# Second half of the first tokens ahead of later weights, a new table of early steps, and the scan mask's flags sent through DRAM

## The chip, the cores and the metric

The kernel runs on one core of a Trainium2 chip, as one launch. The metric is the device time of that launch in microseconds (us); lower is better. Engines: PE is TensorE's matmul, PEld its weight load, DVE is VectorE, ACT is ScalarE, POOL is GpSimd, SP is SyncE (it issues nearly all transfers here).

## What is computed

`x` is 2048 tokens of 448 channels (`L = 2048`, `D = 448`), everything is float32. Two branches read it and a gate mixes them.

```python
g  = sigmoid((x * gate_w).sum(-1, keepdims=True))
# a: a long convolution, K built from 256 complex decays per channel
dt = exp(log_dt); A = -exp(log_A_real) + 1j * A_imag; C = (C_real + 1j * C_imag) * dt[:, None]
K  = 2 * einsum("dn,dnl->dl", C, exp((A * dt[:, None])[:, :, None] * arange(L))).real
a  = causal_convolution(x, K) + x * D_skip
# b: token shift and a channel MLP
h  = gelu(layernorm(x) @ w1)                  # 448 x 448
hs = shift(h, by channel group: +1, -1, +2, -2) @ w2
x1 = x + hs
b  = x1 + gelu(layernorm(x1) @ w3) @ w4       # 448 x 1792, 1792 x 448
out = g * a + (1 - g) * b
```

## The kernel before

**Tiles and units.** The tokens are cut into four blocks of 512 (`TB`), a block into four tiles of 128. TensorE's work is a list of 72 units: 16 units of kind "a" (block b, channel group g; `layernorm(x) @ w1` and the product with `w2`) and then 56 units of kind "d" (block b, hidden tile f of 14; the product with `w3` and the product with `w4`). For each unit `first(n)` (line 478) makes the 512-column product into a bank of PSUM, ACT takes its gelu (line 539) and a rounded copy (line 549), DVE takes the rest (`act_tail`, line 569), and `second(n)` (line 602) multiplies the result by the second weight into four accumulators. Every float32 operand is kept as a rounded high part and a low part (`xh`/`xl`, `w1h`/`w1l`, `uh`/`ul`), so each product is made of up to three: high by high, high by low, low by high. `uh` is used by the first eight of the twelve matmuls of a `second`, `ul` by the last four.

**The order of the steps.** The program order on each engine's queue is written out by hand. `begin()` runs a table, `ORDER`, for units 0 to 3 and a part of units 4 and 5. A word such as `p1:h0a` is one product of unit 1: high weight, slice 0 of the contraction, first half (`a`) of the 512 tokens; `l` is the low weight, `x` the low part of the tokens, a missing letter the whole 512. `s0:20` is one matmul of `second(0)` into accumulator 2. Other words take the next step of a small task: `w` a warm-up matmul on constants (line 902), `m2`, `m0`, `m1`, `m3` the column means of a group of `w1` (lines 930, 914, 866), `c` the centering of the weight by it (line 936, DVE), `h` and `l` its high part (line 939, ACT) and low part (line 942, DVE), `xha`/`xhb` the high part of the first and second half of the first tokens (line 955, ACT), `xla`/`xlb` the low part (line 962, DVE), `sa`, `sb` statistics of a token tile, `ra0` the reciprocal deviation, `ra` its turn into rows on PE, `hd` gelu steps, `cp` copies, `tl` low parts, `ba`, `bm` copies of those rows.

After the table a loop runs over n from 4 to 71. In turn n it issues `first(n + 2)`, the gelu of unit n + 2 and `second(n)`, and between them whatever is registered with `at(n, function, ..., when=...)`, in four lists: `before`, `after`, `between`, `late`. The list `before` runs at the turn's start, right after `act_tail(n + 1)`.

**The first loads.** Before the table `first_loads()` issues the transfers in an order written by hand: on SP and ACT, a column group of `w1` (in `w1r`), the first tokens transposed (`x0` into `r`, its first half in two parts, its second half `r[:, 4 * HW:]` later), token tiles for the statistics (`load_x`), the identity, `w2`, and the next block. Transfers take eight lanes (semaphores) in turn; a transfer is issued only when the one eight before it has landed.

**The scan branch.** The convolution is done in a short form where the decays allow it: four cumulated scans per block and channel slice with coefficients `nu`. `ssm_guard` (turn 33) computes per partition a flag `rk[:, 4:5]`, 1 if the short form is allowed there. `ssm_mask` makes one flag of the 128, writes it to `okm` and copies the coefficients `nuf` into `nu` where it is set. Before, this is a matmul with ones on PE that sums the flags over the partitions (line 734, turn 34, between `first(36)` and `second(34)`), read back by DVE. `ssm_queue` (turn 33) fills the queue of scan steps and issues the loads of the first two blocks, 1 MB each (line 744). From turn 35 (`OWN`) the scan steps run: `ssm_scale` on ACT (line 752) multiplies by `nu`, `ssm_scan` on DVE (line 757), then `ssm_sum`, and `ssm_turn` with its writes (line 775). `ssm_some` hands out scan steps per turn up to a credit. At the end, on every core engine, `okm` is read and a branch runs a general convolution if the flag is 0; with the inputs given it is not run.

**The outputs.** `done(b, j)` writes an output tile once both branches have added to it (line 579); tiles of block 0 are written in two halves. `last_two()` does the last two units and writes the last tile in two parts (line 643). After that SP waits for every lane.

Of the kernel before, what the change touches and what calls it, by code (L numbers as in the profile page):

```python
# [8 lines left out]
F32 = mybir.dt.float32  # L9
# [170 lines left out]
def mixer_and_small_steps(ctx, tc, xs, gg, okm, x, xT, xb, x0, w1, w2, w3, w4, gate, par, logdt, dskip, ident, out):  # L180
# [74 lines left out]
    def first_loads():  # L255
# [16 lines left out]
        load_w1(sp, 1)  # L272
        load_x(1, 2)
# [3 lines left out]
        sp(r[:, 4 * HW:], x0[:, 4 * HW:])  # L277
# [295 lines left out]
    def done(b, j):  # L573
        q = NT * b + j
        parts[q] = parts.get(q, 0) + 1
        if parts[q] == 2:
            for p in range(0, 128, 64 if b == 0 else 128):
                t = slice(p, p + (64 if b == 0 else 128))
                nc.sync.dma_start(out[q * 128 + t.start:q * 128 + t.stop], xs[t, q, :])
# [151 lines left out]

    def ssm_mask():
        p = ps.tile([128, 1], F32, name="misc", bufs=1)
        nc.tensor.matmul(p, one.to_broadcast([128, 128]), rk[:, 4:5], start=True, stop=True)  # L734
        nc.vector.tensor_copy(rk[:, 5:6], p)
        nc.vector.tensor_scalar(okm, rk[:, 5:6].to_broadcast([128, 16]), 127.5, None, op0=OP.is_ge)
        nc.vector.copy_predicated(nu.rearrange("p a b -> p (a b)"), okm, nuf.rearrange("p a b -> p (a b)"))
# [298 lines left out]
    def each(*calls):  # L1036

        for fn, *a in calls:
            fn(*a)
            yield  # L1040

    def more_loads():
# [8 lines left out]
        ws=each((presum,)), m0=each((presum_mean,)), w=each(*((warm_up, 1) for _ in range(5))),  # L1051
# [38 lines left out]
    w w wt xha w wt m2 w xla m2 ws c2 m0 c2 h2 h2 l2 l2 p1:h0a c0 xha xz p1:x0a sk w xz sa0 xla p1:h2a m1 c0  # L1090
    h0 xla sa1 l0 p0:x0a p1:x1a p0:h0a c1 p1:x2a h0 p1:h1a,h3a sa0 ld m3 l0 h1 p0:h3a c3 p0:x2a,l2a,l1a sa2
    p0:x1a p2:h1a sb3 p2:x0a p0:h1a,l3a,h2a h3 p2:h2a l1 p2:h3a pe xhb sb3 p3:x2a sb3 p2:x1a xhb p0:l0a
    p2:l2a p0:h0b p3:h2a xlb p2:h0a sa1 p1:h1b p2:x2a p3:h3a p2:h1b sb3 p0:h2b xlb p0:l0b sa2 p2:h0b p1:x0b
    xlb p3:x1b p0:x2b,h1b l3 p0:l1b p2:x0b wh0 p1:x2b p0:x0b p1:h3b ra0 p0:x1b ra0 p0:h3b p2:x2b ra0 p3:h1b
    xh1 p3:l3a ra0 p3:x2b p2:l0a ra0 p2:l0b ra0 xh1 p1:h0b p3:h2b ra0 p3:l2b p2:x1b ra0 p0:l3b xh1 ra0
    p2:h3b p1:x1b sk p1:h2b wl0 p0:l2b xh1 p3:l1a ra sk uf0 sk p2:l2b xl1 rm p2:l1a p3:x0b uf1 p3:l0b mu0
    p3:x0a sk p4:l1 mu0 p4:h1 sk ad1 p2:h2b hd0 p3:l3b,h0b p4:h3 hd0 mu0 p3:l2a mu1 p2:l1b bm p2:l3a mu1
    p3:h3b hd0 p3:x1a,h1a,l1b hd0 p4:l2 xl1 s0:00 hd0 s0:10 p5:h3 xl1 hd0 p4:x0 s0:01 ba p5:h0 sb7 s0:20 hd0
    hd1 p2:l3b tl0 s0:21 p3:l0a p5:x1 sb7 wh2 mu2 s0:30 p5:x0 cp1 p4:h2 sb5 p3:h0a s0:02 wh1 p4:h0 tl0 s0:11
    sb5 s0:31 tl1 hd2 s0:22 p5:h2 p4:l3 wl2 hd2 p5:h1 hd2 s0:12 sb7 p4:x1 cp2 s1:11,31 sb5 s1:20 cp2 s1:01  # L1100
    sb7 s0:32 sb5 s2:30 tl2 s1:30,10 s2:20 ra1 mu3 s2:00 s1:21 s2:22 ra1 s1:00 wl1 hd3 p4:l0 s2:10 ra1 wh3
    s2:02 ra1 s2:01 ra1 s2:31 hd3 xl1 hd3 s2:11,32,21 ra1 cp3 s2:12 ra1 p4:x2 ra1 wl3 p5:x2 s3:30 uf5 s3:20
    ra1 tl3 s3:00 rn sb9 s3:01 bn s3:12,31 ad5 s3:02 cp3 s3:21,10 mu4 s3:22,32,11 re hd4 re hd4 hd4 mu5 cp4
    re cp4 hd5 tl4 cp5 sb9 re
# [102 lines left out]
    at(34, ssm_mask, when=between)  # L1207
    at(33, ssm_queue)
    for m in (3, 2, 1, 0):
        at(OWN, ssm_scale, 0, 0, m)  # L1210
# [3 lines left out]
    with tc.manual_schedule():  # L1214
        begin()
        for n in range(4, len(units)):
# [23 lines left out]
            if n >= OWN:  # L1240
                ssm_some(n, 3.75 - (2.2 if units[n][2] == NF - 1 else 0.0) - spent)
# [59 lines left out]
```

## Time and profile before

| | before |
|---|---|
| median of three runs | 371.3 us (371.2 to 372.18) |
| time of the profiled execution | 371.42 us |
| its span, first to last instruction | 369.6 us |
| mean granted TensorE clock | 0.997 |
| PE busy | 363.9 us (98%) |
| DVE, ACT, POOL busy | 308.5, 216.1, 63.8 us |
| read from and written to DRAM | 34.74 and 11.01 MB |

The span is the time between the first and the last instruction that the profile shows; the execution's own time is 1.8 us longer. Times in the views count from the span's start. A busy PE is not PE at its peak, so holes and the spacing of equal pieces are read, not the busy share alone.

### The profile page before, as it was taken

How to read it: one execution, taken by the hardware profiler on the slowest of the kernel's cores; microseconds unless marked ns; L12 is line 12 of the kernel's file. 1: busy time of each engine (PE TensorE's matmuls, PEld its weight loads, DVE VectorE, ACT ScalarE, POOL GpSimd, SP SyncE). 2: the span in 40 equal slices, each digit the busy share in tenths (PEclk: the TensorE clock that was granted, in tenths of full speed). 3: DMA queues.
4: the chain of work that ended last, by engine and by line, in shares of the span. 5: the costliest groups of instructions: out<-in, count | busy, mean ns of one | idle time of the engine just before them, and what ended most of it. 6: DMA issues, size and time to landing. Idle time of an engine off the chain costs nothing.

```text
span 369.6 us, 5310 instructions
## 1 busy us (share of the span) xinstructions
PE 363.9 (98%) x1734; PEld 314.8 (85%) x1734; DVE 308.5 (83%) x571; ACT 216.1 (58%) x383; POOL 63.8 (17%) x176
## 2 busy tenths in 40 slices
PE   8999999999999999999999999999999999999995
PEld 5988888888888888888888888888888888888884
DVE  4999979788989997388789899997889999999433
ACT  5887678776674737944373774554656745445220
POOL 1000433000400000110014333324234324000000
PEclk9999999999999999999999999999999999999998
DMA  7994116727938064001833514367485611361213
GB/s 268 394 398 143 48 54 128 160 82 254 381 122 192 2 121 150 0 0 51 192 93 82 84 28 121 86 178 126 86 127 114 177 27 25 72 178 30 66 48 105
DMA packets 88495, 46.14 MB, mean 125 GB/s; under 512 B 67216, under 2 KB 82960, under 8 KB 87824
## 3 DMA queue, kind: packets, MB, share of 16 engines
q1 hardware_dynamic: 88032, 45.27, 45.5%
q10 hardware_dynamic: 432, 0.49, 0.4%
q8 instruction: 15, 0.25, 0.3%
q14 instruction: 16, 0.13, 0.1%
HBM read 34.74 MB, written 11.01 MB: 124 GB/s over the span
## 4 chain that ended last, share of the span: by engine, by line
PE 95%; DMA 3%; SPq 0%; ACT 0%; DVE 0%; issue 0%
PE p L478 48%; PE acc L602 45%; DMA raw<-x_in 2%; DMA w1r<-w_in 1%; PE acc L637 1%; PE misc L363 0%; PE p L637 0%; SPq L246 0%; ACT xh L955 0%; SPq L264 0%; DVE xs L626 0%; PE misc L734 0%
## 5 line engine op out<-in xcount | busy, mean ns | idle before, releaser
L539 ACT ACTIVATE uf<-p 128x512 f32<-128x512 f32 x56 | 33.5, 599 | 113.3 <-PE p L478 113.3
L478 PE MATMUL p<-xh,w3l 128*128 128x512 f32 x224 | 70.1, 394 | 0.0
L478 PE MATMUL p<-xh,w3h 128*128 128x512 f32 x224 | 70.0, 394 | 0.0
L757 DVE TENSOR_TENSOR_SCAN z<-z,carry 128x512 f32<-128x512 f32 x48 | 61.6, 1283 | 4.2 <-POOL z L751 0.5
L602 PE MATMUL acc<-w4l,uh 128*128 128x448 f32 x216 | 56.3, 366 | 0.0
L602 PE MATMUL acc<-w4h,uh 128*128 128x448 f32 x216 | 56.0, 365 | 0.0
L602 PE MATMUL acc<-w4h,ul 128*128 128x448 f32 x216 | 55.8, 364 | 0.0
L569 DVE TENSOR_TENSOR ul<-uf,uh 128x512 fp32r<-128x512 f32 x56 | 38.1, 681 | 20.0 <-ACT uh L549 19.8
L478 PEld LDWEIGHTS p<-xh,w3l 128*128 128x128 f32 x224 | 42.1, 188 | 9.8
L478 PEld LDWEIGHTS p<-xh,w3h 128*128 128x128 f32 x224 | 42.1, 188 | 6.6
L478 PE MATMUL p<-xl,w3h 128*128 128x512 f32 x168 | 47.7, 392 | 0.0
L602 PEld LDWEIGHTS acc<-w4h,uh 128*128 128x128 f32 x216 | 40.5, 188 | 6.0
L602 PEld LDWEIGHTS acc<-w4h,ul 128*128 128x128 f32 x216 | 40.6, 188 | 3.6
L602 PEld LDWEIGHTS acc<-w4l,uh 128*128 128x128 f32 x216 | 40.5, 188 | 3.4
L752 ACT ACTIVATE z<-zs,nu 128x512 f32<-128x512 f32 x64 | 42.3, 710 | 0.2 <-DVE xl L409 0.2
L478 PEld LDWEIGHTS p<-xl,w3h 128*128 128x128 f32 x168 | 31.5, 188 | 7.2
L549 ACT ACTIVATE uh<-uf 128x512 fp32r<-128x512 f32 x56 | 35.4, 633 | 1.8
L751 POOL COPY z<-carry 128x1 f32<-128x1 f32 x48 | 32.7, 692 | 16.0 <-DVE zs L763 15.9
L759 POOL COPY carry<-z 128x1 f32<-128x1 f32 x48 | 13.1, 273 | 105.1 <-DVE z L757 104.4
L344 POOL TENSOR_TENSOR t<-r 128x4 f32<-128x4 f32 (+1 forms) x5 | 3.1, 626 | 117.4 <-DVE r L343 117.4
L757 DVE TENSOR_TENSOR_SCAN z<-z,carry,zero 128x512 f32<-128x512 f32 x16 | 20.0, 1248 | 0.0
L602 PE MATMUL acc<-w2l,uh 128*128 128x448 f32 x64 | 19.9, 367 | 0.0
(207 smaller groups left out, 543.7 us busy)
## 6 DMA issues: line engine op xcount, KB each, us to landing
zs<-xT_in SPq DMA_DIRECT2D x4, 1024.0 KB, 8.1
yd<-yt SPq DMA_DIRECT2D x56, 64.0 KB, 2.0
ysb<-yd SPq DMA_DIRECT2D x16, 224.0 KB, 2.7
raw<-xb_in SPq DMA_DIRECT2D x3, 1032.0 KB, 12.6
raw<-w_in SPq DMA_DIRECT2D x3, 1024.0 KB, 5.6
xd<-xt SPq DMA_DIRECT2D x16, 192.0 KB, 2.1
xr<-xd SPq DMA_DIRECT2D x16, 192.0 KB, 3.1
raw<-w_in SPq DMA_DIRECT2D x3, 896.0 KB, 4.6
```

The source lines that it names most:

```text
L344: eng.tensor_mul(t, y, y)
L478: nc.tensor.matmul(p[:, t0:t1], (wl if w else wh)[:, k, :], (xl if x_ else xh)[:, k, o + t0:o + t1], start=(q == 0 and fresh), stop=stop i ...
L539: nc.scalar.activation(UF[n], P1[n], AF.Gelu_apprx_tanh)
L549: nc.scalar.activation(UH[n], UF[n], AF.Copy)
L569: nc.vector.tensor_sub(UL[n], uf, f32(UH[n]))
L602: nc.tensor.matmul(ACC[j], (UL if p == 2 else UH)[n][:, t], wl if p == 1 else wh, start=first_, stop=last_)
L637: nc.tensor.matmul(acc, (UL if p == 2 else UH)[m][:, t], (wl if p == 1 else wh)[:, c], start=q == last and m == n and p == 0, stop=m > n a ...
L751: nc.gpsimd.tensor_copy(z4[:, m, 0:1], carry[:, k, m:m + 1])
L752: nc.scalar.activation(z4[:, m, 1:], ZS[b][:, k, :], AF.Copy, scale=nu[:, k, m:m + 1])
L757: nc.vector.tensor_tensor_scan(z, z, up, carry[:, k, m:m + 1], OP.add, OP.add)
L759: nc.gpsimd.tensor_copy(carry[:, k, m:m + 1], z[:, TB - 1:])
```

## The change

In `first_loads` the second half of the first tokens is issued earlier, ahead of token tiles 1 to 4 and of group 3 of `w1`. The table `ORDER` is a new one, over the same tasks; it has three `w` steps instead of five. Only the first tile of block 0 is still written in two halves. The flags no longer go through PE: `ssm_tell` (turn 33, after the loads of `ssm_queue`) writes the 128 flags to DRAM, `ssm_hear` (turn 34) reads the 128 numbers back into every partition, and `ssm_mask` (now at the start of turn 35) takes their minimum on DVE. The credit per turn is 3.7 instead of 3.75.

```diff
@@ -270,11 +270,11 @@
         act(xs[:, 0, :], x[0:128])
         sp(r[:, 2 * HW:4 * HW], x0[:, 2 * HW:4 * HW])
         load_w1(sp, 1)
+        sp(r[:, 4 * HW:], x0[:, 4 * HW:])
         load_x(1, 2)
         load_x(2, 3)
         load_w1(sp, 3)
         load_x(3, 5)
-        sp(r[:, 4 * HW:], x0[:, 4 * HW:])
         sp(idt, ident)
         sp(w2r[:, 0], w2[:, 0])
         load_xt(1)
@@ -573,9 +573,10 @@
     def done(b, j):
         q = NT * b + j
         parts[q] = parts.get(q, 0) + 1
+        h = 64 if b == 0 and j < 1 else 128
         if parts[q] == 2:
-            for p in range(0, 128, 64 if b == 0 else 128):
-                t = slice(p, p + (64 if b == 0 else 128))
+            for p in range(0, 128, h):
+                t = slice(p, p + h)
                 nc.sync.dma_start(out[q * 128 + t.start:q * 128 + t.stop], xs[t, q, :])
 
     ADDED = {}
@@ -729,11 +730,21 @@
         nc.vector.tensor_scalar(rk[:, 0:4], rk[:, 0:4], RHO / L, None, op0=OP.is_le)
         nc.vector.tensor_reduce(rk[:, 4:5], rk[:, 0:4], axis=AX.X, op=OP.min)
 
+    OKB = []
+
+    def ssm_tell():
+
+        OKB.append(dr.tile([1, 128], F32, name="okd"))
+        nc.sync.dma_start(OKB[0].rearrange("o p -> p o"), rk[:, 4:5])
+
+    def ssm_hear():
+        OKB.append(big.tile([128, 128], F32, name="okb", tag="lt"))
+        row = OKB[0]
+        nc.sync.dma_start(OKB[1], bass.AP(tensor=row.tensor, offset=row.offset, ap=[[0, 128], [1, 128]]))
+
     def ssm_mask():
-        p = ps.tile([128, 1], F32, name="misc", bufs=1)
-        nc.tensor.matmul(p, one.to_broadcast([128, 128]), rk[:, 4:5], start=True, stop=True)
-        nc.vector.tensor_copy(rk[:, 5:6], p)
-        nc.vector.tensor_scalar(okm, rk[:, 5:6].to_broadcast([128, 16]), 127.5, None, op0=OP.is_ge)
+        nc.vector.tensor_reduce(rk[:, 5:6], OKB[1], axis=AX.X, op=OP.min)
+        nc.vector.tensor_scalar(okm, rk[:, 5:6].to_broadcast([128, 16]), 0.5, None, op0=OP.is_ge)
         nc.vector.copy_predicated(nu.rearrange("p a b -> p (a b)"), okm, nuf.rearrange("p a b -> p (a b)"))
 
     ZZ, ZS = {}, {}
@@ -1048,7 +1059,7 @@
         nc.sync.dma_start(dts[:, 0, :], logdt)
 
     TASKS = dict(
-        ws=each((presum,)), m0=each((presum_mean,)), w=each(*((warm_up, 1) for _ in range(5))),
+        ws=each((presum,)), m0=each((presum_mean,)), w=each(*((warm_up, 1) for _ in range(3))),
         xha=each((x_hi, 0, lh), (x_hi, 2, lh)), xhb=each((x_hi, 0, rh), (x_hi, 2, rh)),
         xla=each((x_lo, 0, 2, lh), (x_lo, 2, 3, lh), (x_lo, 3, 4, lh)),
         xlb=each((x_lo, 0, 2, rh), (x_lo, 2, 3, rh), (x_lo, 3, 4, rh)),
@@ -1087,21 +1098,20 @@
             TASKS[f"mu{n}"] = mul_ops(n)
 
     ORDER = """
-    w w wt xha w wt m2 w xla m2 ws c2 m0 c2 h2 h2 l2 l2 p1:h0a c0 xha xz p1:x0a sk w xz sa0 xla p1:h2a m1 c0
-    h0 xla sa1 l0 p0:x0a p1:x1a p0:h0a c1 p1:x2a h0 p1:h1a,h3a sa0 ld m3 l0 h1 p0:h3a c3 p0:x2a,l2a,l1a sa2
-    p0:x1a p2:h1a sb3 p2:x0a p0:h1a,l3a,h2a h3 p2:h2a l1 p2:h3a pe xhb sb3 p3:x2a sb3 p2:x1a xhb p0:l0a
-    p2:l2a p0:h0b p3:h2a xlb p2:h0a sa1 p1:h1b p2:x2a p3:h3a p2:h1b sb3 p0:h2b xlb p0:l0b sa2 p2:h0b p1:x0b
-    xlb p3:x1b p0:x2b,h1b l3 p0:l1b p2:x0b wh0 p1:x2b p0:x0b p1:h3b ra0 p0:x1b ra0 p0:h3b p2:x2b ra0 p3:h1b
-    xh1 p3:l3a ra0 p3:x2b p2:l0a ra0 p2:l0b ra0 xh1 p1:h0b p3:h2b ra0 p3:l2b p2:x1b ra0 p0:l3b xh1 ra0
-    p2:h3b p1:x1b sk p1:h2b wl0 p0:l2b xh1 p3:l1a ra sk uf0 sk p2:l2b xl1 rm p2:l1a p3:x0b uf1 p3:l0b mu0
-    p3:x0a sk p4:l1 mu0 p4:h1 sk ad1 p2:h2b hd0 p3:l3b,h0b p4:h3 hd0 mu0 p3:l2a mu1 p2:l1b bm p2:l3a mu1
-    p3:h3b hd0 p3:x1a,h1a,l1b hd0 p4:l2 xl1 s0:00 hd0 s0:10 p5:h3 xl1 hd0 p4:x0 s0:01 ba p5:h0 sb7 s0:20 hd0
-    hd1 p2:l3b tl0 s0:21 p3:l0a p5:x1 sb7 wh2 mu2 s0:30 p5:x0 cp1 p4:h2 sb5 p3:h0a s0:02 wh1 p4:h0 tl0 s0:11
-    sb5 s0:31 tl1 hd2 s0:22 p5:h2 p4:l3 wl2 hd2 p5:h1 hd2 s0:12 sb7 p4:x1 cp2 s1:11,31 sb5 s1:20 cp2 s1:01
-    sb7 s0:32 sb5 s2:30 tl2 s1:30,10 s2:20 ra1 mu3 s2:00 s1:21 s2:22 ra1 s1:00 wl1 hd3 p4:l0 s2:10 ra1 wh3
-    s2:02 ra1 s2:01 ra1 s2:31 hd3 xl1 hd3 s2:11,32,21 ra1 cp3 s2:12 ra1 p4:x2 ra1 wl3 p5:x2 s3:30 uf5 s3:20
-    ra1 tl3 s3:00 rn sb9 s3:01 bn s3:12,31 ad5 s3:02 cp3 s3:21,10 mu4 s3:22,32,11 re hd4 re hd4 hd4 mu5 cp4
-    re cp4 hd5 tl4 cp5 sb9 re
+    w w wt xha w wt m2 m2 ws c2 m0 c2 h2 xla h2 sk l2 l2 xha xz p1:h0a c0 p1:x1a xz p1:x0a,h1a sa0 xla m1 c0
+    h0 xla h0 p1:h2a l0 p1:x2a p0:x0a xhb p0:h1a c1 p0:h2a p1:h3a p0:h0a,x2a xhb p0:l0a l0 p1:h0b p0:h3a,l1a
+    xlb h1 p0:h1b ld p1:h2b p0:h2b,x1a,h0b sa0 xlb p1:h1b p2:h0a m3 l1 sa1 p2:x2b c3 p2:x0a sa2
+    p0:l2a,x0b,l1b p2:l1a sb3 p2:x1a,x0b h3 p2:l2b p1:x0b p2:h0b xlb p0:l3a pe sa1 sb3 sb3 p2:x2a p3:x2a,x0a
+    wh0 l3 p3:x0b p0:x1b p2:h2a p1:x1b sa2 p0:l2b p2:h1a sb3 wl0 p2:l0a p3:h1b p1:x2b p0:l0b p3:x2b,l3a ra0
+    xh1 p1:h3b ra0 p0:h3b,x2b ra0 p3:x1a,h3a xh1 ra0 p3:h1a ra0 p0:l3b p3:l0b ra0 p2:x1b xh1 p2:h3a ra0
+    p2:l1b ra0 p2:l0b p3:l1b ra0 p3:h0b xh1 p3:l2b sk p2:l2a,h1b sk rm uf0 sk ra xl1 uf1 p3:l0a mu0 p2:l3b
+    sk p4:l0 mu0 p2:h2b sk p2:l3a ad1 p4:h3 hd0 p4:h0,h2 hd0 mu0 mu1 p3:l2a,l3b mu1 hd0 p4:l2 p5:h2 hd0
+    p3:l1a xl1 p3:h3b hd1 s0:10 p3:x1b p5:h3 sb7 hd0 p4:l1 p3:h0a bm p4:h1 ba tl0 p5:h1 sb5 p2:h3b p5:h0 hd0
+    p3:h2a s0:00 hd0 sb7 cp1 tl0 s0:20 p3:h2b s0:11 mu2 wh2 s0:02,30,12 sb5 tl1 hd2 s0:21,01 p4:x0 sb7 hd2
+    s0:22 hd2 s1:10,00 sb5 s0:31 cp2 s1:20 sb7 s0:32 sb5 wl2 p5:x0 wh1 s1:30 p4:l3 wh3 ra1 tl2 s1:01,31
+    s2:20 ra1 s2:30 mu3 s2:00,12,22 ra1 wl1 hd3 s1:11 s2:10,02 ra1 s1:21 xl1 hd3 cp2 s2:31 hd3 s2:01,11 ra1
+    xl1 s2:32 cp3 s2:21 p5:x1 ra1 p4:x1 cp3 ra1 s3:00 ra1 wl3 p4:x2 p5:x2 s3:10 ra1 sb9 uf5 s3:30 rn tl3
+    s3:01 bn s3:31,20 ad5 s3:22,32,02 mu4 s3:12,21,11 re hd4 mu5 hd4 hd4 re cp4 re hd5 tl4 cp4 cp5 re sb9
     """
 
     def products(n, codes):
@@ -1204,8 +1214,10 @@
         for m in range(4):
             at(q[m], ssm_moment, k, m)
     at(33, ssm_guard)
-    at(34, ssm_mask, when=between)
+    at(34, ssm_hear)
+    at(35, ssm_mask, when=before)
     at(33, ssm_queue)
+    at(33, ssm_tell)
     for m in (3, 2, 1, 0):
         at(OWN, ssm_scale, 0, 0, m)
 
@@ -1238,7 +1250,7 @@
             if n + LAG < len(units) and n not in (6, 10):
                 act_copy(n + LAG)
             if n >= OWN:
-                ssm_some(n, 3.75 - (2.2 if units[n][2] == NF - 1 else 0.0) - spent)
+                ssm_some(n, 3.7 - (2.2 if units[n][2] == NF - 1 else 0.0) - spent)
             run(late, n)
             if n < len(units) - 2 and n not in (7, 11):
                 second(n)
```

## Prediction

> **What bounds the kernel now.** I read the page first, then the PE table by stretches, then the chain that ended last at its two ends and at the mask, and last the rows of single transfers.
>
> ```profile
> span 369.6 us, 5310 instructions
> PE 363.9 (98%) x1734; PEld 314.8 (85%) x1734; DVE 308.5 (83%) x571; ACT 216.1 (58%) x383; POOL 63.8 (17%) x176
> L539 ACT ACTIVATE uf<-p 128x512 f32<-128x512 f32 x56 | 33.5, 599 | 113.3 <-PE p L478 113.3
> ```
>
> TensorE is the bound, almost everywhere; ACT's gelu (L539, 0.6 each) is idle 113.3 us just waiting for PE's products. A table of stretches shows where it is not:
>
> ```profile
> 5.00:7.14 2.14, 1.81 (x13) 1.53 (x11) 1.66 (x6) 0.69 (x3) 0.27 (x2) 1.00 1.02 379
> 7.14:13.00 5.86, 5.80 (x50) 5.35 (x50) 5.36 (x14) 5.18 (x15) 0.26 (x2) 1.00 1.04 380
> 13.00:34.00 21.00, 20.98 (x127) 19.12 (x128) 20.14 (x57) 16.49 (x39) 0.71 (x4) 1.00 0.86 324
> 34.00:365.00 331.00, 331.00 (x1538) 287.10 (x1536) 280.44 (x494) 191.63 (x326) 61.64 (x154) 1.00 0.42 106
> ```
>
> Columns: stretch, length, busy time and instructions of PE, weight loads, DVE, ACT, POOL, granted clock, DMA share, GB/s. From 34 us to 365 us PE has no hole at all. So an edit can gain only in three places: before 34 us, in PE work that is taken out, and in the 4.6 us from 365 to the end of the span. The early chain:
>
> ```profile
> 5.77 6.54 DMA raw<-x_in
> 12.33 0.64 ACT xh L955
> 13.02 4.67 PE p L478 x37
> ```
>
> The second half of the first tokens is issued at 5.77, lands at 12.3, is rounded by ACT and releases PE at 13.02; from there on half products follow each other at 4.67/37 = 0.126 us.
>
> **The change part by part.**
>
> *Mask off TensorE.* The chain around the mask:
>
> ```profile
> 175.24 2.55 PE p L478 x11
> 180.22 2.55 PE p L478 x11
> 182.77 0.12 PE misc L734 x2
> 182.89 2.55 PE acc L602 x12
> 185.44 2.56 PE p L478 x11
> 197.97 2.43 PE acc L602 x12
> ```
>
> A unit takes 180.22 - 175.24 = 4.98; the one with the mask takes 185.44 - 180.22 = 5.22. Taking the two matmuls out gives -0.24, whole, since PE is the bound there.
>
> *What the mask costs instead.* The flags go out (tell) and come back (hear) through SP, after the two 1 MB loads of `ssm_queue`, and the first mask step now waits on DVE for hear.
>
> ```profile
> L744 SPq DMA_DIRECT2D zs<-xT_in x2: 613/622/632, 178.5 to 179.1; - x2
> DMA to landing us min/median/max: 6.7/8.3/9.8
> 13.80 2.85 SPq L659 DMA_DIRECT2D gr<-gate_in  x1
> 16.69 0.52 SPq L1047 DMA_DIRECT2D dsk<-dskip_in  x1
> gr<-gate_in SPq DMA_DIRECT2D x1, 224.0 KB, 14.2
> dsk<-dskip_in SPq DMA_DIRECT2D x1, 2.0 KB, 11.5
> DMA to landing us min/median/max: 1.8/2.0/3.9
> 186.21 0.29 DVE L410 TENSOR_TENSOR xh<-xr,xh 64x128 fp32r<-64x128 f32 x1
> 187.82 1.25 DVE L757 TENSOR_TENSOR_SCAN z<-z,carry,zero 128x512 f32<-128x512 f32 x1
> 192.17 0.67 DVE L569 TENSOR_TENSOR ul<-uf,uh 128x512 fp32r<-128x512 f32 x1
> 185.29 2.57 ACT L752 ACTIVATE z<-zs,nu 128x512 f32<-128x512 f32 x4 [0.17 <-DVE xl L409]
> ```
>
> (The first landing line is of the zs loads, the second of the 64 KB writes of line 775.) The loads land last at 179.1 + 9.8 = 188.9. Small transfers do not overtake: dsk has 2 KB, yet it lands at 28.2, 0.2 behind gr (28.0). So tell lands near 189.1, not 2 us after its issue. Only then SP may issue hear; at 2.0, hear lands at 191.2. DVE stands still from 186.5 (end of the L410 row) until then; three short steps, some 0.6 (an estimate: the 0.29 of L410 for the first, less for two on 16 columns), end the mask at 191.8. Behind it on DVE queue the statistics, then the scans, which began 187.82 - 186.5 = 1.3 after that point: now 193.1, 5.3 late. The L569 step that followed the scans at 192.17 comes at 197.5 and ends at 198.1. On ACT the four scalings (2.57) wait as well, and behind them unit 37's gelu (0.6) and a copy of the same size, 1.2 more: 191.9 + 2.6 + 1.2 = 195.7.
>
> PE is the one who could wait. Its second product for unit 37 stood at 197.97, 0.24 earlier now: it takes the copy first (195.7, 2.0 in hand) and the L569 result after 8 of 12 matmuls, 197.7 + 1.6 = 199.3 (1.2 in hand). So the delay of 5.3 is hidden, with a margin of 1.2; DVE then works the delay off, being 85% busy in the long stretch (280.44/331). I take 0. SP stands from 180 to 191; what is queued on it behind hear carries results of these same later steps, so that costs nothing more.
>
> By the Trainium skill (DMA: Bandwidth & Descriptors, the section on the anatomy of one DMA) each transfer has a fixed 2 us, mostly the wait for the target memory's write receipt. By that, an estimate, hear would land at 188.9 + 4.0 = 192.9 and PE would wait some 0.5. The 0.2 between gr and dsk speaks against 2 us for one that follows another closely, though both are loads; no row shows a 4-byte write to DRAM.
>
> *The last transfer's lane.*
>
> ```profile
> L643 SPq DMA_DIRECT2D out_dram<-xs x2: 348/386/423, 365.0 to 365.5; - x2
> DMA to landing us min/median/max: 2.2/2.3/2.4
> L60 SPq EVENT_SEMAPHORE  x8: 17/17/17, 367.7 to 368.2; - x8
> ```
>
> At the end SP waits for eight lanes one after the other. The first of these waits ends at 367.7, just when the last transfer lands (365.5 + 2.2): the last transfer is on the first lane, and seven more waits stand behind it, 368.2 - 367.7 = 0.5. Transfers take the lanes in turn. The change has three output halves fewer and two transfers more, one fewer in all, so the last moves back to the eighth lane; the other seven waits are then over when it lands. Gain -0.5, on the path.
>
> *The early table.* PE's products are the same; two warm-up matmuls go.
>
> ```profile
> 5.31 0.61 PE L902 MATMUL pw<-const-bfloat16-1.0 128*128 128x512 bf16 x1
> 5.74 0.35 PE L930 MATMUL pm<-ws,cm 128*128 128x64 f32 x2
> 7.14 0.39 PE L478 MATMUL p<-xh,w1d 128*128 128x256 f32 x1 [0.33 <-DVE w1d L942]
> 7.83 1.05 PE L866 MATMUL pm<-w1r,cm 128*128 128x128 f32 x8
> 12.54 0.40 PE L478 MATMUL p<-xh,w1l 128*128 128x256 f32 x2
> 4.93 0.70 DVE L962 TENSOR_TENSOR xl<-raw,xh 128x520 fp32r<-128x520 f32 x1
> 6.13 0.48 DVE L936 TENSOR_TENSOR w1r<-w1r,pm 128x128 f32<-128x128 f32 x2 [0.30 <-PE pm L930]
> 6.79 0.49 DVE L942 TENSOR_TENSOR w1d<-w1r,w1d 128x128 fp32r<-128x128 f32 x2 [0.18 <-ACT w1d L939]
> 2.12 0.43 SPq L264 DMA_DIRECT2D w1r<-w_in  x1
> w1r<-w_in SPq DMA_DIRECT2D x1, 256.0 KB, 5.4
> ```
>
> First product. The warm-up at 5.31 stood before the second mean; without it the mean and DVE's centering (6.13) come some 0.4 earlier, 5.7. But the 0.70 step of L962, which stood before them, now stands between centering and L942: 5.7 + 0.45 + 0.6 = 6.75 against 6.79. The first product moves from 7.14 to about 7.1: -0.05. The warm-ups gone give nothing more; their place is covered by this DVE chain.
>
> Second half. It goes behind the 2.12 transfer, which lands at 7.5. Its 512 KB at 380 GB/s (the 7.14 row) take 1.4: 8.9 instead of 12.3. After the landing PE was released 0.7 later (12.3 to 13.02): 9.6. In the new table 13 half products and the eight means stand ahead of its first use: 7.1 + 13 x 0.126 + 0.8 = 9.5 (0.8 is the 1.05 of L866 less the drain of its last matmul, some 0.25). A wait of 0.1 is left, for the 0.24 that goes (12.54 + 2 x 0.12 to 13.02).
>
> Later weights. Token tiles 1 and 2 and group 3 of w1 (704 KB) now follow: 8.9 + 1.9 = 10.8, for means that stand ten half products on, at 9.6 + 1.3 = 10.9: just in time. Tiles 3 and 4 land near the old 12.3 in sum, ahead of their statistics.
>
> Gelu of unit 0. Its last pieces on ACT now stand behind unit 1's gelu and two copies of rows. The second products of its second half stand earlier among PE's steps than that order delivers; I bound the wait by 0 and 0.4 and take 0.2, and 0.1 for the first product of unit 4, which waits for a bank.
>
> Sum: -0.05 - 0.24 + 0.1 + 0.2 + 0.1 = +0.1. Bounds: of the 50 matmuls of the 7.14 row, 25 are half products, 16 means at 0.1, eight are tiny: about 5.0 of 5.86, so at most 0.86 more can be won, -0.9; and the transfers 0.5 late with all waits whole give +0.8.
>
> *No cost.* 3.7 for 3.75 puts a few DVE scan steps one unit later, the last turn too; the last outputs then fall among the closing additions, which have idle time between them. Three output halves joined save SP issues that nobody waits for.
>
> **Total.** Against the profiled execution (371.42): -0.24 - 0.5 + 0.1 = -0.64, 370.8. The median before lies 0.1 lower (371.3), so 370.7. About 0.3% (1.1 us) is what a measurement of this kernel can tell from no change.
>
> **The rivals.**
>
> Slower: *the returned flags come too late.* The place is unit 37's second product. It decides once hear lands after 192.4, and each us beyond costs one. At the largest row of a 64 KB transfer for both ways (3.9) it lands at 196.7: 4.3 of waiting, 375.0; over 0.3% from about 194.1. For it: DVE and ACT both stand behind that one wait, and no row shows tell. Against: the chip's queue is empty by 189. Chance 0.10.
>
> Slower: *a colder TensorE.* Ten warm-ups open the kernel, and PE now rests about 1 us before the first product instead of 0.6. If half products then ran at twice 0.126 for the 25 that stand there, 3 us are lost: 373.8. Against: the granted clock reads 1.00 in every stretch. Chance 0.05. The Trainium skill (TensorE: Matmul & The Clock Gate, Part 1) has a window of about 3.4 us of activity behind such a drop, which a rest of 1 us need not fill.
>
> Faster: *the new table closes the early holes.* Then the -0.9 holds: 371.3 - 0.74 - 0.9 = 369.7; over 0.3% from -0.4 on. For it: the one transfer in the early chain is moved. Against: DVE and ACT feed those products and are over 88% busy there (5.36 and 5.18 of 5.86). Chance 0.28.
>
> *The late weights decide.* Group 3 lands at 11.4 instead of 10.8: +0.6, 371.3. Chance 0.08. *The lane does not move* (the halves or the order of lanes count otherwise): 371.2. Chance 0.04.
>
> **How the numbers follow.** Forecast 0.45; with the last two, no change 0.57; faster 0.28; slower 0.15. The range goes from the best early bound, 369.7, to 372.0, which takes in the worst early bound (371.4) and a small wait at the mask; left out are most of the slower cases and a little below, under 0.2.
>
> **What would show it.** The lines to look at: the chain without L734 and all units near it at 4.98; hear landing near 191.2, the scans from 193, PE without a hole at 198; SP's eight waits with only the last after the landing; the first product at 7.1 and the second half landed by 9. A PE wait on DVE or ACT near 198, or a hole over 0.5 us between 9 and 24, would make it wrong.

## The result: slower by 1.6%, and the profile after

The changed kernel takes 378.15 us in the median of four runs (376.88 to 378.37), the kernel before 371.74 in the same session (371.2 to 372.28). The ratio is 1.0164, with a 95% interval of 1.0145 to 1.0183. The forecast was 370.7, in a range from 369.7 to 372.0: wrong in sign. The profiled execution after took 376.88, with a span of 375.1; that is 5.5 more than the 369.6 before. It is the fastest of the four; the other three took 378.0 to 378.4, so the views below account for 5.5 of the loss, and 1.1 to 1.5 us that the others lose besides are not in them.

Three lines of the page after: the span, and PE and the granted clock in 40 slices of 9.4 us.

```profile
span 375.1 us, 5302 instructions
PE   7999999999999999999995999999999999999996
PEclk9999999999999999999998999999999999999998
```

PE now has a hole in the middle, in the slice from 197 to 206 us (the 5), and the clock dips there too (the 8). The chain that ended last, near that place (start, length, what), comes next:

```profile
180.31 13.49 DMA okd<-rk
...
193.86 4.02 DMA okb<-okd
...
198.64 2.56 ACT z L763 x4
201.20 0.49 ACT uf L539
...
201.71 0.64 ACT uh L549
...
202.39 4.26 PE acc L603 x12
206.65 2.55 PE p L478 x11
209.21 2.43 PE acc L603 x12
```

The chain leaves PE here. It follows the flags: tell (`okd<-rk`) takes 13.49 from issue to landing, hear (`okb<-okd`) 4.02 more, then come the mask, the four scalings on ACT, unit 37's gelu and its copy, and only then that unit's second product. The same place among PE's own instructions (start, duration of one, count; in brackets the rest before it and what ended it), and then in stretches of time (columns as in the prediction's table):

```profile
197.44 0.85 PE L478 MATMUL p<-xl,w3h 128*128 128x512 f32 x3
202.39 1.81 PE L603 MATMUL acc<-w4h,uh 128*128 128x448 f32 x4 [4.10 <-ACT uh L549]
```

```profile
203.00:206.00 3.00, 3.00 (x10) 2.65 (x9) 2.79 (x9) 2.97 (x6) 1.89 (x4) 0.52 0.00 0
206.00:210.00 4.00, 4.00 (x20) 3.41 (x19) 3.90 (x8) 3.08 (x7) 1.91 (x4) 1.00 0.07 21
```

PE rests 4.10 us, and ACT's copy ends the rest. After it the granted clock is 0.52 until 206, and back at 1.00 from then on: the twelve matmuls of unit 37 take 4.26 instead of the 2.43 of the next second product in the chain, 1.83 more. 4.10 and 1.83 make 5.9. The product that is gone takes 0.24 off that, the lane 0.5 and a last write that landed in 1.8 instead of 2.2 another 0.4; the 0.7 that then lacks to 5.5 lies mostly in the early part: the first group of eleven products (`PE p L478 x11`) starts at 34.72 instead of 34.14.

At the start, PE's first product and the wait that followed; at the end, the last writes with their landing, and SP's waits for the eight lanes:

```profile
6.93 0.39 PE L478 MATMUL p<-xh,w1d 128*128 128x256 f32 x1 [0.67 <-DVE w1d L953]
8.18 1.16 PE L877 MATMUL pm<-w1r,cm 128*128 128x128 f32 x8 [0.51 <-DMA w1r<-w_in]
```

```profile
L644 SPq DMA_DIRECT2D out_dram<-xs x2: 332/372/411, 371.5 to 371.9; - x2
DMA to landing us min/median/max: 1.8/1.9/2.0
```

```profile
L60 SPq EVENT_SEMAPHORE  x8: 17/17/17, 372.9 to 373.7; - x8
```

The wait for the second half of the tokens is gone, and a wait of 0.51 for a group of `w1` stands at 8.18 instead. The last write lands at 371.9 + 1.8 = 373.7, where the last of SP's eight waits ends now, not the first.

### The profile page after: what moved, and what is told of

Read it like the earlier page. It is cut to its first block, busy times and chain, and to the rows that moved or that the text cites. A ratio compares the mean times of both kernels' runs of the same rounds, so it can differ in the third digit from the quotient of the medians.

```text
span 375.1 us, 5302 instructions
## 1 busy us (share of the span) xinstructions
PE 365.4 (97%) x1730; PEld 315.0 (84%) x1730; DVE 307.7 (82%) x571; ACT 215.7 (58%) x383; POOL 65.3 (17%) x176
## 4 chain that ended last, share of the span: by engine, by line
PE 89%; DMA 6%; DVE 2%; ACT 1%; SPq 0%; issue 0%
PE p L478 45%; PE acc L603 42%; DMA okd<-rk 4%; DMA w1r<-w_in 2%; DMA okb<-okd 1%; PE acc L638 1%; ACT z L763 1%; PE pm L877 1%; PE misc L363 0%; PE p L638 0%; DVE mw L712 0%; ACT uh L549 0%; DVE ul L569 0%; ACT uf L539 0%; DVE mw L714 0%
## 5 line engine op out<-in xcount | busy, mean ns | idle before, releaser
L478 PE MATMUL p<-xh,w3l 128*128 128x512 f32 x224 | 70.1, 394 | 0.0
L478 PE MATMUL p<-xh,w3h 128*128 128x512 f32 x224 | 70.0, 394 | 0.0
L603 PE MATMUL acc<-w4h,uh 128*128 128x448 f32 x216 | 56.8, 369 | 4.1 <-ACT uh L549 4.1
L478 PEld LDWEIGHTS p<-xh,w3l 128*128 128x128 f32 x224 | 42.1, 188 | 9.8
L478 PE MATMUL p<-xl,w3h 128*128 128x512 f32 x168 | 47.7, 392 | 0.0
L478 PEld LDWEIGHTS p<-xh,w3h 128*128 128x128 f32 x224 | 42.1, 188 | 6.6
L478 PEld LDWEIGHTS p<-xl,w3h 128*128 128x128 f32 x168 | 31.5, 188 | 7.2
L603 PE MATMUL acc<-w2h,uh 128*128 128x448 f32 x64 | 20.1, 371 | 0.0
```

What stands on the lines that cost most here:

```text
L478: nc.tensor.matmul(p[:, t0:t1], (wl if w else wh)[:, k, :], (xl if x_ else xh)[:, k, o + t0:o + t1], start=(q == 0 and fresh), stop=stop i ...
L603: nc.tensor.matmul(ACC[j], (UL if p == 2 else UH)[n][:, t], wl if p == 1 else wh, start=first_, stop=last_)
```

## The experiments

Each ratio is against the kernel before, measured alongside on the same chip. In the code, `...` marks lines left out. The first four kernels take the change apart.

**mask_only.** The kernel before, with tell, hear and the new mask alone:

```diff
... (ssm_tell, ssm_hear and the new ssm_mask, as in the change)
-    at(34, ssm_mask, when=between)
+    at(34, ssm_hear)
+    at(35, ssm_mask, when=before)
     at(33, ssm_queue)
+    at(33, ssm_tell)
```

> The kernel before with one part of the change alone: the flags through DRAM (tell in turn 33 after the two 1 MB loads, hear in turn 34, the mask at the start of turn 35). Theory M (the round trip of the flags holds DVE and ACT until about 198 us and PE waits): PE has a hole of 4 to 5 us before the second product of unit 37, the nine matmuls after it run at about 0.37 us instead of 0.20, and the time is 5 to 7 us over the kernel before (two more transfers also move the last lane by two, which gives 0 to 0.1). Rival E (the early table and the loads cost the most): within 1 us of the kernel before, no hole near 198.

Measured: 378.45 us, ratio 1.0169 (1.0142 to 1.0195). This part alone carries the whole loss. Its chain:

```profile
180.31 14.08 DMA okd<-rk
...
203.50 4.85 PE acc L602 x12
208.34 3.08 PE p L478 x11
```

This profiled execution is the slowest of its four (379.9), and both terms are larger in it than above: PE rests 5.21, and the clock is still at 0.58 between 206 and 210, so unit 37's second product and the first product behind it take 4.85 and 3.08 instead of 2.43 and 2.55, 2.95 more.

**mask_undone.** The changed kernel with the old mask on PE, and output halves chosen (`j < 3`) so that the last transfer stays on the last lane:

```diff
-        h = 64 if b == 0 and j < 1 else 128
+        h = 64 if b == 0 and j < 3 else 128
... (ssm_tell and ssm_hear out, ssm_mask as before)
-    at(34, ssm_hear)
-    at(35, ssm_mask, when=before)
+    at(34, ssm_mask, when=between)
     at(33, ssm_queue)
-    at(33, ssm_tell)
```

> The changed kernel with the mask back on TensorE (turn 34) and no flags through DRAM; three tiles of block 0 in halves instead of one, so that the last transfer stays on the eighth lane. Theory M: no hole near 198, the time falls by 5.5 to 7 us against the changed kernel, to within 0.7 us of the kernel before: +0.6 from the early stage, -0.5 from the lane. Rival E: it stays 3 us or more above the kernel before.

Measured: 371.61 us, ratio 1.0001 (0.9988 to 1.0013). Without the round trip the hole and the loss are gone: the same from the other side. The credit of 3.7 is in this kernel too, so it costs nothing that the time shows.

**early_only.** The kernel before with the new order of loads, the new table, and three warm-ups instead of five.

```diff
         load_w1(sp, 1)
+        sp(r[:, 4 * HW:], x0[:, 4 * HW:])
...
-        sp(r[:, 4 * HW:], x0[:, 4 * HW:])
...
-    ORDER = """ (the table of before)
+    ORDER = """ (the new table)
```

> The kernel before with the early part alone: the second half of the first tokens issued earlier, the new table, three warm-up steps in it instead of five. Theory M: +0.3 to +0.9 us against the kernel before, because group 1 of w1 lands about 0.6 us later and its means wait for it. Rival E: +4 us or more. A rival to the first (the later landing in the one profile was chance): 0 to -0.5 us, with group 1 landing at 7.5 us as before.

Measured: 372.43 us, ratio 1.0014 (1.0 to 1.0027): some 0.5 us slower, at the edge of what the interval tells from no change. The profiled execution is the fastest of the ten (371.25). In it group 1 of `w1` lands at 7.84 and PE waits 0.3 us for it; that this wait is what the typical execution loses is not shown.

**lane_only.** The kernel before with the fourth tile of block 0 written whole, one output half less, so that there is one transfer fewer in all:

```diff
-            for p in range(0, 128, 64 if b == 0 else 128):
-                t = slice(p, p + (64 if b == 0 else 128))
+            h = 64 if b == 0 and j < 3 else 128
+            for p in range(0, 128, h):
+                t = slice(p, p + h)
```

> The kernel before with one output half fewer (the fourth tile of block 0 is written whole), nothing else. If the last transfer's lane is worth what the eight closing waits show: -0.5 us, seven of the eight closing waits over before the last landing. If the waits overlap with something else at the end: 0.

Measured: 371.05 us, ratio 0.999 (0.9977 to 1.0003). The interval still takes in no change; the profile shows the piece itself:

```profile
L644 SPq DMA_DIRECT2D out_dram<-xs x2: 332/374/416, 365.5 to 365.9; - x2
DMA to landing us min/median/max: 2.0/2.1/2.2
```

```profile
L60 SPq EVENT_SEMAPHORE  x8: 17/17/17, 366.9 to 367.9; - x8
```

From the last landing (365.9 + 2.0 = 367.9) to the end of the span (369.3) it is 1.4 us; before it was 1.95 (landed 367.69, span to 369.64). In mask_undone and pieces, where the last transfer is on the last lane too, it is 1.4 again.

The next four ask whether the flags are late because of their place in the queue, and what the cold clock costs.

**tell_first.** The changed kernel with tell and hear ahead of the two 1 MB loads, in turn 33:

```diff
-    at(34, ssm_hear)
     at(35, ssm_mask, when=before)
-    at(33, ssm_queue)
     at(33, ssm_tell)
+    at(33, ssm_hear)
+    at(33, ssm_queue)
```

> The changed kernel with tell and hear moved ahead of the two 1 MB loads in turn 33, flags computed where they were. Theory M: tell is issued near 180 and hear lands between 184 and 189, before 192.4, so the 5 us that DVE then stands still are hidden and PE has no hole near 198: 6 to 7 us less than the changed kernel; the loads are issued 2 to 6 us later and the scans start near 191 to 194. Rival L (the margin before unit 37 is smaller than the prediction worked out): PE waits 1 us or more near 198 though hear lands before 192.4.

Measured: 375.36 us, ratio 1.0093 (1.0066 to 1.012). Tell no longer stands behind 2 MB, and still takes 8.3 (its issue and its landing):

```profile
L738 SPq DMA_DIRECT2D okd<-rk x1: 338/338/338, 180.2 to 180.2; - x1
DMA to landing us min/median/max: 8.3/8.3/8.3
```

Hear, issued at 188.5, takes 5.6 and lands at 194.15, and the loads issued after it land at 197.5 and 200.6. The expectation, hear by 189 and no hole, was missed. What PE waits for is another thing here than in the changed kernel, though: the mask is done at 194.9, but the scalings on ACT start at 197.60, when the first load has landed (first line, of the chain; second line, of PE's own).

```profile
188.91 8.60 DMA zs<-xT_in
201.35 1.86 PE L603 MATMUL acc<-w4h,uh 128*128 128x448 f32 x4 [2.82 <-ACT uh L549]
```

After this rest of 2.82 the granted clock is 0.56 from 202 to 205.

**flags_early.** The changed kernel with the flags worked out and told at the end of turn 32, heard in turn 33:

```diff
... (the three flag steps of ssm_guard are moved into ssm_flags)
-    at(34, ssm_hear)
+    at(32, ssm_flags)
+    at(32, ssm_tell)
+    at(33, ssm_hear)
     at(35, ssm_mask, when=before)
     at(33, ssm_queue)
-    at(33, ssm_tell)
```

> The changed kernel with the three flag steps of the guard taken out and run at the end of turn 32, tell right behind them, hear in turn 33 ahead of the two 1 MB loads; the mask stays at the start of turn 35. Theory M (the flags come back too late because they queue behind the loads, and PE waits): tell is issued near 173, both ways are over by 184 at the latest, DVE does not wait at the mask, no hole on PE near 198, the time falls by 6 to 7 us to within 0.6 us of the kernel before. Rival D (it is having the mask on DVE at turn 35, ahead of the statistics, the scalings and the scans, that delays unit 37, whenever the flags land): a hole of 2 us or more stays.

Measured: 372.8 us, ratio 1.0028 (1.0007 to 1.0049). Most of the loss is gone. But tell takes 8.9 on a queue that holds next to nothing else, and the fetches of the next tokens' tile (`xr`), issued just behind it, land with it (a view of the transfers from 174 to 188 us; columns: KB each, median us to landing):

```profile
xr<-xd SPq DMA_DIRECT2D x4, 32.0 KB, 10.0
okd<-rk SPq DMA_DIRECT2D x1, 0.5 KB, 8.9
```

The same fetch takes 2.2 to 3 where no tell is ahead. Through that the `zs` loads and the scans come late (195.0 instead of 187.82), and DVE is behind with the scans up to unit 44, of which the second product is late: PE has a rest of 0.7 that ends at 234.28, 0.15 after DVE's first addition out of the finished accumulators is over (L616; its row merges three), which stands behind the scans (DVE's instructions):

```profile
232.28 1.28 DVE L770 TENSOR_TENSOR_SCAN z<-z,carry 128x512 f32<-128x512 f32 x1
233.48 1.84 DVE L616 SCALAR_TENSOR_TENSOR xs<-acc,gs,xs 128x448 f32<-128x448 f32 x3
```

**flags_early_old_table.** The same place for the flags in the kernel before (old table, old loads), with halves for tile 0 alone.

```diff
... (ssm_flags, ssm_tell, ssm_hear, the new ssm_mask; halves for j < 1)
-    at(34, ssm_mask, when=between)
+    at(32, ssm_flags)
+    at(32, ssm_tell)
+    at(33, ssm_hear)
+    at(35, ssm_mask, when=before)
```

> The kernel before (old loads, old table, old credit) with the mask off PE as in flags_early and with one tile of block 0 in halves (the last transfer on the eighth lane). If the parts add: -0.24 for the two matmuls that leave PE and -0.5 for the lane, so -0.7 us against the kernel before and the fastest kernel of all; no hole near 198. Rival (the DVE wait or the early flags cost something that the closing lane hides): 0 or more.

Measured: 372.42 us, ratio 1.0021 (1.0007 to 1.0035), where a gain was expected: a miss. Tell took 8.4, the fetches behind it 9.5 to 10.6, and PE had a rest of 0.5 that ends at 233.35, again 0.15 after the end of DVE's first addition (233.20). The 0.5 is less than the 1.5 between expectation and result, and the profiled execution (371.6) is one of the fastest of the ten, so part of the miss stays open. In none of the three places tried did the queue have room for a transfer that holds the others for 8 us.

**fill.** The changed kernel with 24 idle matmuls of 512 columns in the hole, so that PE does not rest:

```diff
+    def ssm_fill():
+        p = ps.tile([128, TB], F32, name="misc", bufs=1)
+        for _ in range(24):
+            nc.tensor.matmul(p, warm[:, 0:128], warm, start=True, stop=True)
...
+    at(37, ssm_fill, when=late)
```

> The changed kernel with 24 warm-up matmuls of 512 columns on PE in turn 37, ahead of the second product of unit 37, where PE has its hole. Theory C (TensorE's clock is halved by the 4.5 us of rest, and that is 1.7 us of the loss): the matmuls after the hole follow each other at 0.20 instead of 0.37 us, and the time falls by 0.8 to 1.9 us against the changed kernel (24 x 0.22 = 5.2 us of filling can run over the wait by up to 0.8). Rival W (the slow matmuls wait for their inputs, one by one): they stay at 0.37 us and the time does not fall.

Measured: 378.09 us, ratio 1.0172 (1.0146 to 1.0198): no gain, where 0.8 to 1.9 was expected. In the profile (of the fastest of its four, 376.48) the clock does hold:

```profile
198.14 5.19 PE misc L748 x23
203.34 2.43 PE acc L603 x12
205.77 2.55 PE p L478 x11
208.32 2.43 PE acc L603 x12
```

The second product is back at 2.43, and at the next one PE is 0.89 ahead of the changed kernel (208.32 against 209.21): the idle matmuls ran 0.95 longer than the hole of the changed kernel (203.34 against 202.39), which eats half of the 1.83. Here the flags were back earlier, and the copy that PE needs was done at 201.7, so the filling outlasted its own hole by 1.6. At 238.45 PE waits again, for DVE's adding of the accumulators, and is 0.61 ahead (239.06 in the changed kernel). So the cold clock's share is seen in the profile, but these 24 matmuls do not turn it into time; whether fewer would, and where the rest went, the runs do not show.

The next three ask why tell takes 8 us, and whether the change pays without that; the last one returns to the loads.

**probe.** The kernel before, with four transfers added on SP where it has little else to do:

```diff
+        if i == 0:      # 4 bytes from each of 128 partitions to DRAM
+            sp(PB[0].rearrange("o p -> p o"), one)
+        elif i == 1:    # 512 bytes from each to DRAM
+            sp(PB[1], idt)
+        elif i == 2:    # 128 partitions read the same 512 bytes
+            sp(PB[2], bass.AP(tensor=row.tensor, offset=row.offset, ap=[[0, 128], [1, 128]]))
+        else:           # 128 partitions read 128 rows of 512 bytes
+            sp(PB[3], PB[1])
...
+    for i in range(4):
+        at(27 + i, probe, i, when=late)
```

> The kernel before with four added transfers on SP's queue, one at the end of each of turns 27 to 30, where the queue is nearly empty: 128 floats from 128 partitions written to DRAM (4 bytes each), 64 KB written to DRAM in rows of 512 bytes, 128 partitions that all read the same 512 bytes of DRAM, and 64 KB read in 128 different rows of 512 bytes. Theory S (the small pieces make the write slow): the first takes some 8 us, as the tell did alone (8.31, 8.44 and 8.89 us in three kernels), the second 2 to 3 us, and the fourth 2 to 2.5 us. Theory W (any write to DRAM from 128 partitions takes that long): the first and the second both take 8 us or more. On the way back, theory B (one row read by all is slow): the third takes 3.2 us or more, as the hear did on an otherwise empty queue (3.20 to 5.63 us), the fourth about 2; against it, both take the same.

Measured (one profiled execution, 371.34 us). The view of the transfers in that stretch (KB, median us from issue to landing):

```profile
pk<-par_in SPq DMA_DIRECT2D x1, 1024.0 KB, 6.8
pbb<-idt SPq DMA_DIRECT2D x1, 64.0 KB, 10.2
pbc<-pba SPq DMA_DIRECT2D x1, 64.0 KB, 3.2
pbd<-pbb SPq DMA_DIRECT2D x1, 64.0 KB, 1.9
pba<-one SPq DMA_DIRECT2D x1, 0.5 KB, 10.5
```

The first two did not stand alone: a load of 1 MB (`pk`) was just ahead, and lands at 144.84. The 4-byte write lands at 138.44 + 10.49 = 148.93, 4.1 after it; the write of 64 KB, issued at 138.92, lands at 149.10, only 0.17 later with 128 times the bytes. So this run does not tell the two theories apart: the second write may be slow by itself or late behind the first. The kernel before can. It has writes to DRAM in larger pieces, those of line 775 (512 pieces of 128 bytes from 32 partitions, on its page):

```profile
yd<-yt SPq DMA_DIRECT2D x56, 64.0 KB, 2.0
```

Those of line 434 (128 pieces of 256 bytes, one from each of 128 partitions) take 1.8 to 3.8, 1.9 in the median of 16. So neither 128 partitions nor 128 pieces or more make a write slow, and theory W falls; that the probe's 64 KB write was held up behind the 4-byte one, as the fetches were in flags_early, fits this. On the way back, in this one execution, 128 reads of one row take 3.2 and of 128 rows 1.9.

**pieces.** The changed kernel, its places in the order unchanged; only the form of tell is another. Each flag is copied along 32 columns and the 32 x 32 blocks are transposed, so that 4 partitions hold 32 flags each:

```diff
+        f = big.tile([128, 4, 32], F32, name="fl", tag="lt")
+        nc.vector.tensor_copy(f[:, 0, :], rk[:, 4:5].to_broadcast([128, 32]))
+        nc.vector.transpose(f[:, 1, :], f[:, 0, :])
         OKB.append(dr.tile([1, 128], F32, name="okd"))
-        nc.sync.dma_start(OKB[0].rearrange("o p -> p o"), rk[:, 4:5])
+        nc.sync.dma_start(OKB[0].rearrange("o (a c) -> (o a) c", c=32), f[0:128:32, 1, :])
```

> The changed kernel with the flags turned on VectorE first (each flag copied along 32 columns, and the 32 x 32 blocks transposed), so that the tell writes 4 pieces of 128 bytes instead of 128 of 4 bytes; its place in the order stays. VectorE has two more small instructions. Theory S: the tell lands within 1 us of the zs loads ahead of it (188.8 in the changed kernel), at about 189.8, the hear takes 4 us and lands at 193.8, the hole ahead of unit 37's second product shrinks from 4.26 us to under 0.5 (it began with a hear of 193.6 by the changed kernel: 197.87 less 4.26), no halved clock behind it: 372.3 us, at the level of the kernel before to 0.2% above. Theory W: the tell still lands at about 194 and the time stays at 378.

Measured: 371.57 us, ratio 0.9993 (0.9982 to 1.0004). The whole loss is gone with this one edit. The two added steps on DVE, then the issue and landing of hear, then the stretch of time in which the hole was:

```profile
179.78 0.18 DVE L738 COPY fl<-rk 128x32 f32<-128x32 f32 x1
180.00 0.21 DVE L739 STREAM_TRANSPOSE fl<-fl 128x32 f32<-128x32 f32 x1
```

```profile
L746 SPq DMA_DIRECT2D okb<-okd x1: 341/341/341, 189.3 to 189.3; - x1
DMA to landing us min/median/max: 2.8/2.8/2.8
```

```profile
198.00:206.00 8.00, 8.00 (x39) 7.07 (x38) 7.69 (x19) 7.43 (x13) 2.85 (x8) 1.00 0.25 64
```

SP issues hear as soon as tell has landed. That is now at 189.3, 0.5 after the loads (188.8), so a write of 512 bytes in 4 pieces hardly costs anything behind them, where 128 pieces cost 5.0 (193.80). Hear lands at 192.16, below the 192.4 from which the prediction had PE wait, and PE has no hole. (The hole that the expectation puts at 4.26 was 4.10; 4.26 is the length of the product behind it.) What is left of the change is then no gain that the interval can tell: the two gains, 0.24 and 0.5, stand against some 0.5 of the early part.

**pieces_early_old_table.** The best of what was seen: the kernel before with its old table and loads, the flags early as in flags_early_old_table, and tell in 4 pieces.

> The kernel before with its old table and old order of loads, the mask off TensorE, the flags worked out at the end of turn 32, the tell there in 4 pieces of 128 bytes, the hear in turn 33 ahead of the zs loads, and whole blocks of the first tokens written out from block 1 on. Theory S: the tell takes 2 to 3 us instead of 8.44, the xr fetches behind it are back at 2 to 3 us instead of 9.5 to 10.6, the zs loads land as in the kernel before, so neither a hole near 198 nor one near 232 is left, and the time falls by the masking product and the tail, 0.24 + 0.5: 0.2% under the kernel before. Theory W: as with 128 pieces, 0.2% above the kernel before.

Measured: 370.86 us in the median of 11 runs, ratio 0.9972 (0.9962 to 0.9981). It beats both kernels, by a little more than the 0.2% expected. Its profiled execution is the slowest of the eleven (374.01 us). In its middle the chain of waits holds nothing but PE's products, and the fetches behind tell (`xr`) take 2.2 to 2.9, as expected (tell's own landing is missing in this trace):

```profile
193.52 2.55 PE p L478 x11
196.06 2.43 PE acc L603 x12
```

What it lost, it lost before 21 us. The second half of the first tokens landed at 14.17 instead of 12.31; PE rested 0.70 for a weight and then 0.81 for these tokens, and behind these two short rests the granted clock was at half (the chain, and a stretch of time):

```profile
14.87 6.17 PE p L478 x37
16.00:19.00 3.00, 3.00 (x16) 3.00 (x15) 2.59 (x12) 2.60 (x6) 0.00 (x0) 0.50 1.05 392
```

The same 37 products took 4.67 before; late landing and low clock make 3.4 together (21.04 against 17.68).

**loads_only.** The kernel before, with the new order of loads but the old table:

```diff
         load_w1(sp, 1)
+        sp(r[:, 4 * HW:], x0[:, 4 * HW:])
...
-        sp(r[:, 4 * HW:], x0[:, 4 * HW:])
```

> The kernel before with only the new order of the loads (the second half of the first tokens ahead of the later weights), under the old table of steps, which asks for the halves in the old order. With the order and the table together the time was 1.0014 of the kernel before. If the order is what costs it (later weights landing later), this one is as slow or slower, 0.1% to 0.5% above, with waits for w1 or w2 pieces in the first 15 us; if the table is, this one is within 0.1%.

Measured: 373.08 us, ratio 1.0034 (1.0017 to 1.005): slower, as the theory of the later weights had it.

```profile
11.04 1.16 PE L866 MATMUL pm<-w1r,cm 128*128 128x128 f32 x8 [1.20 <-DMA w1r<-w_in]
```

Group 3 of `w1` lands at 10.99 here and at 9.32 before. The old table wants it at 9.44; the new one wants it later, which by the medians takes back more than half of the loss. The two intervals overlap, so the share of the table is only indicated.

## Why the prediction was wrong, point by point

- **Mask off PE, -0.24: right.** L734 is gone, and the products follow each other at 2.55 + 2.43 = 4.98 on both sides.
- **The round trip, taken at 0: this is the step that failed, and it carries the sign.** "So tell lands near 189.1" was the wrong term: it landed at 193.80. The reasoning from `dsk` behind `gr` held for a load; it was carried over to a write of 4 bytes from each of 128 partitions, of which the prediction itself said that no row shows it. tell_first and flags_early show that this write takes 8.3 to 8.9 without 2 MB ahead of it, and pieces, which changes nothing but its form, brings the landing to 189.3. Writes of as many or more pieces of 128 or 256 bytes take 2.0 and 1.9, so it is the 4-byte form; whether the size of a piece alone does it, or that all 128 go to the same 512 bytes of DRAM, no run tells apart. Hear was taken at 2.0 and took 4.0; probe shows 3.2 for the same row read by all and 1.9 for different rows. That is 4.7 and 2.0 too little, 6.7 in sum, against a margin of 1.2.
- **The bound on it was too low as well.** "The largest row of a 64 KB transfer for both ways (3.9)" gave 196.7; the landing was at 197.87. A row of another form of transfer is no upper bound. The 2 us of the Trainium skill (DMA: Bandwidth & Descriptors, the section on the anatomy of one DMA) gave 192.9 and was too small too; that section fits it to transfers issued from GpSimd, while these are issued from SP. What bore on it stands in the same page's specifications: below 512 bytes a transfer is not at line rate, because it becomes a read-modify-write. The traces agree in the direction for 4-byte pieces (8.3 to 8.9 us for 512 bytes in all). They show no such price for pieces of 128 bytes, where tell in 4 pieces lands 0.5 behind the loads and the writes of line 775 take 2.0. That the slow form does a read-modify-write, no run shows.
- **The slower rival: right in mechanism and place, wrong in size and chance.** It named the wait of DVE and ACT for the flags, unit 37's second product, and 192.4 as the point. By its rule 197.87 costs 5.5; the rest was 4.1, so the point was nearer 193.8. That its 4.3 of waiting is close to 4.1 is luck: the flags came 1.2 later than it took, and the point lay 1.4 later. With pieces, 192.16 cost nothing. Its chance of 0.10 was far too small for a kind of transfer that no row showed.
- **The cold clock: put in the wrong place.** The prediction looked for it at the start and priced it there. In the changed kernel it came behind the hole instead, 1.83 us that no rival had (2.95 in mask_only's slower execution). The Trainium skill (TensorE: Matmul & The Clock Gate, Part 1) has the clock halved after one idle window of some 3.4 us and restored after a busy one. The changed kernel's trace agrees: after a rest of 4.10 the granted clock is 0.52, and full again at 206, 3.6 after the restart. Two other traces show that a shorter rest is no safety: 0.56 after 2.82 in tell_first, and 0.50 after rests of 0.70 and 0.81 close together in pieces_early_old_table. That one is at the start of the kernel, so the rival was possible there, and "a rest of 1 us need not fill" the window is no reason to rule it out.
- **The lane, -0.5: right.** From the last landing to the end of the span 1.95 became 1.4, in lane_only and in the changed kernel.
- **The early part, +0.1 with bounds from -0.9 to +0.8: inside, at the worse side.** early_only costs 0.14% (0 to 0.27%), some 0.5 us. The waits put at 0.1, 0.2 and 0.1 (the second half, the gelu of unit 0, the first product of unit 4) do not show among PE's waits. The first product came at 6.93 (forecast 7.1), the second half landed at 9.46 (8.9), group 3 at 11.34 (10.8): the transfers were half a microsecond later than reckoned. The wait that is left is for group 1 of `w1` (0.51), which landed at 8.13 instead of the 7.5 taken over from before; with the old order of loads it landed at 7.83 in lane_only and 8.11 in mask_only, so this part is not due to the order. The faster rival fell: the transfer that was moved ahead puts later weights back, and loads_only shows what that costs under the old table.
- **"SP stands from 180 to 191; ... that costs nothing more": the time was wrong.** In the changed kernel SP stood until 193.9; a cost of that by itself does not show there. What the early variants show is another cost: not SP's waiting, but the transfers behind tell, which land with it.

## What to carry to other kernels

A value per partition that goes through DRAM should be turned into a few long pieces first: here a copy and a transposition of 0.4 us on VectorE took a transfer of 8 us off the queue, and with it 1.7% of the time. Where the trace shows no transfer of the same form (bytes per piece, direction, same row or different rows), its price is open upward, and the forecast must say so in its chances. A delay that is hidden on the bound engine by a margin still fills the queue of the engine beside it: look where that one is next needed.

## What the hardware showed

- A write of 128 times 4 bytes to DRAM took 8.3, 8.4 and 8.9 us in three kernels, and fetches issued behind it on the same queue took 10 us instead of 2.2 to 3. In 4 pieces of 128 bytes the same 512 bytes landed 0.5 after the loads ahead of them; 512 pieces of 128 bytes took 2.0.
- 128 partitions reading one row of 512 bytes took 2.8 to 5.6 us (the 5.6 with 2 MB issued right behind it), where 128 different rows took 1.9 in the one execution that had both.
- After a rest of 4.1 us TensorE ran at a granted clock of 0.52 for the next twelve matmuls; with the rest filled it ran on at 1.00. A rest of 2.8, and two of 0.7 and 0.8 close together, were followed by 0.56 and 0.50 as well.
- SP's waits for the eight lanes at the end come one after the other: with the last transfer on the first lane they cost 0.5 us more than with it on the last.
